# Where the row sums of a softmax get their small constant: GpSimd or ScalarE

## The chip, the cores and the metric
The kernel runs on one core of a Trainium2 chip. The core has a matrix engine (TensorE, PE in the profile, with PEld for the loading of its weights), VectorE (DVE), ScalarE (ACT), GpSimd (POOL) and SyncE (SP), which here issues most of the transfers between HBM and the core's memory SBUF. Each engine works through its own list of instructions in order, and waits on semaphores for the others. The metric is the device time of one execution, in microseconds; the median of several executions is what counts.

## The reference
An attention with a learned position bias is followed by a gated feed-forward layer. With 4 batches, 8 heads, S = 576 positions, heads of 64, and then 2304 tokens of width 512 with an inner width of 1536:
```python
scores = scale * np.matmul(q, k.transpose(0, 1, 3, 2))
...
scores = scores + bias.transpose(2, 0, 1)[None, :, :, :]
scores = scores - np.max(scores, axis=-1, keepdims=True)
attn = np.exp(scores)
attn = attn / (np.sum(attn, axis=-1, keepdims=True) + 1e-09)
return np.matmul(attn, v).astype(np.float32)
...
a = x @ w_a
b = x @ w_b
return (a * b @ w_out).astype(np.float32)
```
`x` is the attention's output, its heads side by side. The constant of the title is the 1e-9 that is added to each row's sum before the division.

## The kernel before
The attention is cut into 32 units (two chunks of positions, 4 batches, 4 pairs of heads) and these into 144 tiles, numbered n, of 128 rows by 576 columns of scores. One tile goes through these steps:

- TensorE multiplies q and k into a score buffer `qk` (L504 and L481 for the first 32 tiles, L490 after, L471 for the tail tile of a unit). One score buffer is used up to tile 50; after that two alternate.
- `soft1(n)`: VectorE's L518 adds the bias, scales, writes `p` to SBUF and keeps each row's minimum `mn`. With its read the score buffer is free for the next tile. Then ScalarE's L523 takes the exponential of `p` in place and leaves the row sums in `sm`; in the profile this is an ACTIVATE and an ACTIVATION_READ_ACCUMULATOR.
- `soft2(n)`, called one tile later in the program: GpSimd's L567 adds 1e-9 to `sm` and, from unit 12 (tile 48) on, divides by PS = 2^14; VectorE's L568 takes the reciprocal.
- Tiles 0 to 47: GpSimd's L573 multiplies `p` by the reciprocal, TensorE transposes it (L585, `tp`), ScalarE copies the result out (L590, L595).
- Tiles 48 to 143 (`split_turn`): GpSimd's L553 writes the normalised tile as 16-bit numbers `ph`, VectorE's two L555 write the remainder beside it, and SyncE issues a transposing transfer L561 of `ph` into `pt`.
- `pv` (L613) multiplies v and the transposed tiles of a unit; ScalarE's L626 and VectorE's L628 write the result into `x`.

The buffers `p` (three) and `sm`, `mn` (four each) rotate. Beside the attention TensorE does the feed-forward layer of the batch that is ready: the products `ab` (L715), which ScalarE scales (L723, `asb`), VectorE multiplies (L725, `g`), ScalarE and GpSimd split in two parts (L739 `gh`, L740 `gl`), and the output products (L764). Until some 37 us the position bias is built (`psta`), until some 165 us the weights are converted, by ScalarE (L264, L307), VectorE (L266, L267, L270) and GpSimd (L304, L308); the other half of the bias follows from 240 to 320 us. The attention ends at some 640 us, and the rest is feed-forward.

The order of TensorE's instructions is written by hand, by generators that are merged step by step (`tc.manual_schedule` for PE alone). The order of all other engines is set by the scheduler, which plays the program through with its own idea of each instruction's length and places each instruction when it takes its inputs to be ready. So a row added to one engine can change the order on the others.

Of the kernel before, what the change touches and what calls it, by code (L numbers as in the profile page):

```python
# [13 lines left out]
AF = mybir.ActivationFunctionType  # L14
ALU = mybir.AluOpType
# [15 lines left out]
PS = float(2 ** 14)  # L31
# [3 lines left out]
TILES = []  # L35
# [12 lines left out]
NF = 3 * NP  # L48
# [4 lines left out]
def attention_moe(ctx, tc, q0d, q1d, kd, vd, idn, wp, wa, wb, wo, lsw, lg, rl, out):  # L53
    nc = tc.nc
# [456 lines left out]
    def soft1(n):  # L511
        ps = st.pop(("qk", n))
        bt = st.pop(("bias", n))
        pool, bufs = att, 3
        p = pool.tile([128, S], F32, tag="p", name="p", bufs=bufs)
        mn = att.tile([128, 1], F32, tag="mn", name="mn", bufs=4)
        sm = att.tile([128, 1], F32, tag="sm", name="sm", bufs=4)
        ttr = nc.vector.tensor_tensor_reduce(  # L518
            out=p.rearrange("p (a n) -> p a n", a=2), in0=ps[:, :, :HB], in1=bt.rearrange("p (a n) -> p a n", a=2),
            op0=ALU.add, op1=ALU.min, scale=-0.125, scalar=3.0e38, accum_out=mn,  # L520
        )
        ttrs.append(ttr)
        exps.append(nc.scalar.activation(p, p, AF.Exp, bias=mn, scale=-1.0, accum_out=sm))  # L523
        st["p", n] = (p, sm)

    def pv_first(n, pool):
# [36 lines left out]
    def soft2(n):  # L563
        u, t = TILES[n]
        p, sm = st.pop(("p", n))
        rc = sm
        nc.gpsimd.tensor_scalar(out=sm, in0=sm, scalar1=1e-9, scalar2=1.0 / (PS if u >= NF else 1.0), op0=ALU.add, op1=ALU.mult)  # L567
        nc.vector.reciprocal(out=rc, in_=sm)  # L568
        if u >= NF:
            split_turn(n, p, rc)  # L570
            return
        pns.append(
            nc.gpsimd.tensor_scalar(out=p, in0=p, scalar1=rc, scalar2=1.0, op0=ALU.mult, op1=ALU.mult)  # L573
        )
        st["pn", n] = p
# [59 lines left out]
    def attn_steps():  # L635
        vgen = [None]
        for n in range(NT + 4):
# [7 lines left out]
            if n < NT:  # L645
                soft1(n)
# [47 lines left out]
            if 1 <= n <= NT:  # L694
                soft2(n - 1)
# [297 lines left out]
```

## Time and profile before

| | us |
|---|---|
| median of the runs (757.84 to 761.88) | 759.58 |
| the profiled execution, its span | 760.0 |
| TensorE busy | 704.6 |
| VectorE busy | 498.8 |
| ScalarE busy | 446.3 |
| GpSimd busy | 329.1 |

The span is that of one profiled execution, from its first instruction to its last. Read first the busy times, which tell which engine has little room; then the waits of that engine by what they waited for; then the timeline at the longest of them, from the waiting instruction backwards: the last thing in brackets is the idle time before an instruction and what ended it. An engine that is idle and not waited for costs nothing. The granted clock (PEclk) is TensorE's clock as a share of 2.4 GHz; its lower level is 1.2 GHz, half of that.

### The profile page before, as it was taken

How to read it: one execution, taken by the hardware profiler on the slowest of the kernel's cores; microseconds unless marked ns; L12 is line 12 of the kernel's file. 1: busy time of each engine (PE TensorE's matmuls, PEld its weight loads, DVE VectorE, ACT ScalarE, POOL GpSimd, SP SyncE). 2: the span in 40 equal slices, each digit the busy share in tenths (PEclk: the TensorE clock that was granted, in tenths of full speed). 3: DMA queues.
4: the chain of work that ended last, by engine and by line, in shares of the span. 5: the costliest groups of instructions: out<-in, count | busy, mean ns of one | idle time of the engine just before them, and what ended most of it. 6: DMA issues, size and time to landing. Idle time of an engine off the chain costs nothing.

```text
span 760.0 us, 15571 instructions
## 1 busy us (share of the span) xinstructions
PE 704.6 (93%) x5451; PEld 531.9 (70%) x5451; DVE 498.8 (66%) x1204; ACT 446.3 (59%) x1005; POOL 329.1 (43%) x477
## 2 busy tenths in 40 slices
PE   7778898899899999999889989999999999999997
PEld 2245465578787556687677768878778887888886
DVE  6767688849986578675788778878887772110200
ACT  6878887867875687754456456545655553422310
POOL 3437668855873133232545445524553452411200
PEclk9989999989999999999999999999999999999999
DMA  8898767477744888789999999999999974000001
GB/s 260 299 371 272 242 218 214 148 235 252 252 154 127 209 183 218 193 212 180 225 245 248 274 255 229 243 240 245 238 254 248 213 158 112 17 1 28 3 14 42
DMA packets 178163, 147.69 MB, mean 194 GB/s; under 512 B 125092, under 2 KB 138148, under 8 KB 178084
## 3 DMA queue, kind: packets, MB, share of 16 engines
q1 hardware_dynamic: 170928, 130.92, 68.2%
q10 hardware_dynamic: 5876, 10.93, 5.2%
q0 software_dynamic: 1280, 4.84, 1.8%
q8 instruction: 43, 0.70, 0.4%
q14 instruction: 36, 0.29, 0.1%
HBM read 101.15 MB, written 17.18 MB: 156 GB/s over the span
## 4 chain that ended last, share of the span: by engine, by line
PE 36%; issue 17%; DVE 15%; POOL 12%; ACT 10%; DMA 9%; SPq 1%; POOLq 0%; DVEq 0%; ACTq 0%
PE ab L715 15%; PE o L764 10%; POOL ph L553 5%; DMA bias<-bias_d 3%; POOL gl L740 3%; DMA pt<-ph 3%; DVE p L518 3%; PE pv L613 3%; PE psta L153 3%; DVE ph L555 2%; ACT p L523 2%; PE qk L490 2%; DVE w16t L267 2%; DVE wt L270 2%; POOL sm L567 2%
## 5 line engine op out<-in xcount | busy, mean ns | idle before, releaser
L715 PEld LDWEIGHTS <-w16t 128*128 128x128 f16 x2592 | 248.3, 98 | 47.2 <-issue 14.3
L715 PE MATMUL ab<-x,w16t 128*128 128x256 f16 x2304 | 273.2, 275 | 2.6 <-DVE g L725 1.0
L523 ACT ACTIVATE p<-p,mn 128x576 f32<-128x576 f32 x144 | 111.7, 776 | 138.7 <-DVE mn L518 117.4
L555 DVE SCALAR_TENSOR_TENSOR ph<-p,sm,ph 128x64 f16<-128x64 f32 x192 | 98.7, 554 | 34.1 <-POOL ph L553 32.0
L764 PE MATMUL o<-wos,gh 128*128 128x512 f32 x384 | 120.7, 395 | 0.0
L518 DVE CUSTOM_DVE_ANT_0 p<-qk,bias 128x576 f32<-128x576 f32 x144 | 107.7, 751 | 17.0 <-PE tp L585 5.6
L567 POOL TENSOR_SCALAR sm<-sm 128x1 f32<-128x1 f32 x144 | 42.1, 292 | 173.6 <-ACT p L523 169.3
L740 POOL TENSOR_TENSOR gl<-g,gh 128x256 fp32r<-128x256 f32 x96 | 75.1, 783 | 93.3 <-ACT gh L739 90.4
L553 POOL TENSOR_SCALAR ph<-p,sm 128x576 f16<-128x576 f32 x96 | 82.0, 854 | 52.5 <-DVE sm L568 39.7
L725 DVE SCALAR_TENSOR_TENSOR g<-ab,wv,asb 128x256 f32<-128x256 f32 x84 | 40.2, 479 | 73.0 <-ACT asb L723 73.0
L490 PE MATMUL qk<-ks,qs 128*128 128x288 f32 x384 | 72.9, 312 | 11.9 <-DVE mn L518 11.7
L764 PEld LDWEIGHTS o<-wos,gh 128*128 128x128 f32 x384 | 69.4, 188 | 16.0 <-issue 2.8
L764 PE MATMUL o<-wos,gl 128*128 128x512 f32 x192 | 75.0, 391 | 0.0
L490 PEld LDWEIGHTS qk<-ks,qs 128*128 128x128 f32 x384 | 55.8, 188 | 25.1 <-DVE mn L518 16.7
L739 ACT CAST gh<-g 128x256 fp32r<-128x256 f32 x96 | 38.3, 399 | 33.2 <-DVE g L725 32.8
L573 POOL TENSOR_SCALAR p<-p,sm 128x576 f32<-128x576 f32 x48 | 44.1, 920 | 28.5 <-DVE sm L568 23.9
L723 ACT ACTIVATE asb<-ab,wv 128x256 f32<-128x256 f32 x84 | 39.4, 469 | 27.6 <-PE ab L715 27.3
L568 DVE RECIPROCAL sm<-sm 128x1 f32<-128x1 f32 x144 | 23.1, 160 | 44.5 <-POOL sm L567 42.5
L407 DVE TENSOR_TENSOR ks<-rk,ks 64x576 fp32r<-64x576 f32 x48 | 44.9, 934 | 3.7 <-ACT ks L406 1.7
L613 PE MATMUL pv<-pt,vs 128*64 128x320 f16 (+1 forms) x560 | 41.8, 302 | 0.0
L585 PE MATMUL tp<-idn,p 128*128 128x128 f32 x240 | 37.1, 287 | 4.8 <-ACT ptf L590 4.0
L764 PEld LDWEIGHTS o<-wos,gl 128*128 128x128 f32 x192 | 36.0, 188 | 7.8
(102 smaller groups left out, 956.0 us busy)
## 6 DMA issues: line engine op xcount, KB each, us to landing
bias<-bias_d SPq DMA_DIRECT2D x128, 288.0 KB, 3.6
rv<-vd SPq DMA_DIRECT2D x32, 320.0 KB, 4.2
rk<-kd SPq DMA_DIRECT2D x24, 288.0 KB, 3.5
wraw<-wa SPq DMA_DIRECT2D x12, 512.0 KB, 7.0
wraw<-wb SPq DMA_DIRECT2D x12, 512.0 KB, 5.3
wraw<-wo SPq DMA_DIRECT2D x12, 512.0 KB, 4.5
bias_d<-bo ACTq DMA_DIRECT2D x20, 295.5 KB, 3.9
bias_d<-bo POOLq DMA_DIRECT2D x16, 295.5 KB, 7.0
```

The costliest lines, as they stand in the source:

```text
L407: nc.vector.tensor_tensor(out=ks[ol, j], in0=rk[sl], in1=ks[sl, j].bitcast(F32), op=ALU.subtract)
L490: nc.tensor.matmul(ps[:, hf, :HB], a, b[:, hf * HB:hf * HB + HB], start=(x == 0), stop=(x == len(prods) - 1))
L518: ttr = nc.vector.tensor_tensor_reduce(out=p.rearrange("p (a n) -> p a n", a=2), in0=ps[:, :, :HB], in1=bt.rearrange("p (a n) -> p a n", a=2),
L523: exps.append(nc.scalar.activation(p, p, AF.Exp, bias=mn, scale=-1.0, accum_out=sm))
L553: nc.gpsimd.tensor_scalar(out=ph[:, :S], in0=p, scalar1=rc, scalar2=1.0, op0=ALU.mult, op1=ALU.mult)
L555: ins = nc.vector.scalar_tensor_tensor(out=ph[:, o:o + c1 - c0], in0=p[:, c0:c1], scalar=rc, in1=ph[:, c0:c1], op0=ALU.mult, op1=ALU.subtract,
L567: nc.gpsimd.tensor_scalar(out=sm, in0=sm, scalar1=1e-9, scalar2=1.0 / (PS if u >= NF else 1.0), op0=ALU.add, op1=ALU.mult)
L573: nc.gpsimd.tensor_scalar(out=p, in0=p, scalar1=rc, scalar2=1.0, op0=ALU.mult, op1=ALU.mult)
L613: nc.tensor.matmul(ps[64 * j:64 * j + 64, o:o + N], v[:, j, :], p[:, j * N:j * N + N], start=(x == 0), stop=(x == len(prods) - 1),)
L715: nc.tensor.matmul(ab[:, j], w16[nm, f][:, pw, kk, :], xs[px][:, kk, :], start=(x % (3 * KC) == 0), stop=(x % (3 * KC) == 3 * KC - 1),)
L740: nc.gpsimd.tensor_tensor(out=gl, in0=g, in1=gh.bitcast(F32), op=ALU.subtract)
L764: nc.tensor.matmul(o, g[:, sl], wos[f][:, p], start=(f == 0 and x == 0), stop=(f == FC - 1 and x == 2))
```

## The change
In `soft1`, right after the exponential, ScalarE takes a copy of `sm` with a scale and a bias, so that `sm` holds (sum + 1e-9), divided by PS from tile 48 on. GpSimd's L567 in `soft2` is gone. The values are the same but for rounding. The program gives the copy one call behind the exponential; where it stands on ScalarE is the scheduler's choice, as before. Lines behind the new ones carry numbers that are one or two higher: the copy is L525, the reciprocal L569, the remainders L557, asb L724, g L726, gh L740.

```diff
--- before.py
+++ after.py
@@ -521,6 +521,8 @@
         )
         ttrs.append(ttr)
         exps.append(nc.scalar.activation(p, p, AF.Exp, bias=mn, scale=-1.0, accum_out=sm))
+        unit = PS if TILES[n][0] >= NF else 1.0
+        nc.scalar.activation(sm, sm, AF.Copy, bias=1e-9 / unit, scale=1.0 / unit)
         st["p", n] = (p, sm)
 
     def pv_first(n, pool):
@@ -564,7 +566,6 @@
         u, t = TILES[n]
         p, sm = st.pop(("p", n))
         rc = sm
-        nc.gpsimd.tensor_scalar(out=sm, in0=sm, scalar1=1e-9, scalar2=1.0 / (PS if u >= NF else 1.0), op0=ALU.add, op1=ALU.mult)
         nc.vector.reciprocal(out=rc, in_=sm)
         if u >= NF:
             split_turn(n, p, rc)
```

TensorE's order is the same before and after. ScalarE has 144 rows more and GpSimd 144 fewer; on VectorE about half of the rows move, most by one or two.

First VectorE, where the reduces of tiles 69 and 70 stand (`L518 ISA p,mn` is the reduce, `ISA mn` its read of the minimum, the two SCALAR_TENSOR_TENSOR rows on `ph` the remainders of one tile, here tile 68 first). Before:
```order
L518 ISA p,mn<-qk,bias 128x576
L518 ISA mn 128x1
L555 SCALAR_TENSOR_TENSOR ph<-p,sm,ph 128x64
L555 SCALAR_TENSOR_TENSOR ph<-p,sm,ph 128x512
L518 ISA p,mn<-qk,bias 128x576
L518 ISA mn 128x1
L568 RECIPROCAL sm<-sm 128x1
L725 SCALAR_TENSOR_TENSOR g<-ab,wv,asb 128x256
```
The reduce of tile 70 is the second one here; the remainders of tile 68 stand ahead of it. In the changed program the same place on VectorE reads:
```order
L518 ISA p,mn<-qk,bias 128x576
L518 ISA mn 128x1
L442 SCALAR_TENSOR_TENSOR vs<-rv,vs_452,vs 128x640
L569 RECIPROCAL sm<-sm 128x1
L518 ISA p,mn<-qk,bias 128x576
L518 ISA mn 128x1
L569 RECIPROCAL sm<-sm 128x1
L557 SCALAR_TENSOR_TENSOR ph<-p,sm,ph 128x64
L557 SCALAR_TENSOR_TENSOR ph<-p,sm,ph 128x512
L726 SCALAR_TENSOR_TENSOR g<-ab,wv,asb 128x256
```
The reduce of tile 70 stood behind the remainders of tile 68, and now stands ahead of them, behind a row on `vs` and the reciprocal of tile 68.

VectorE again, around the reduce of tile 40, among the rows that convert weights (`wu`, `wt`). Before:
```order
L568 RECIPROCAL sm<-sm 128x1
L267 SCALAR_TENSOR_TENSOR wu<-wraw,wu 128x512
L270 SCALAR_TENSOR_TENSOR wt<-wt,wu 128x512
L628 SCALAR_TENSOR_TENSOR x_2506<-pv,vs_2249,x_2505 128x256
L266 TENSOR_SCALAR wu<-wt 128x512
L267 SCALAR_TENSOR_TENSOR wu<-wraw,wu 128x512
L518 ISA p,mn<-qk,bias 128x576
L518 ISA mn 128x1
L725 SCALAR_TENSOR_TENSOR g<-ab,wv,asb 128x256
```
The reduce stands behind two rows on `wu`. In the changed program the same place on VectorE reads:
```order
L267 SCALAR_TENSOR_TENSOR wu<-wraw,wu 128x512
L270 SCALAR_TENSOR_TENSOR wt<-wt,wu 128x512
L629 SCALAR_TENSOR_TENSOR x_2508<-pv,vs_2251,x_2507 128x256
L569 RECIPROCAL sm<-sm 128x1
L266 TENSOR_SCALAR wu<-wt 128x512
L726 SCALAR_TENSOR_TENSOR g<-ab,wv,asb 128x256
L518 ISA p,mn<-qk,bias 128x576
L518 ISA mn 128x1
L267 SCALAR_TENSOR_TENSOR wu<-wraw,wu 128x512
```
The long row on `wu` from `wraw` has moved from ahead of the reduce to behind it; the reciprocal of tile 39 and the row on `g` have moved ahead of it.

Last ScalarE, at the exponentials of tiles 71 to 73 (`p,sm<-p,mn`; `ks` and `qs` are parts of the next unit's k and q). Before:
```order
L523 ACTIVATE p,sm<-p,mn 128x576
L723 ACTIVATE asb<-ab,wv 128x256
L739 CAST gh<-g 128x256
L523 ACTIVATE p,sm<-p,mn 128x576
L723 ACTIVATE asb<-ab,wv 128x256
L406 CAST ks<-rk 64x576 x2
L418 CAST qs<-rq 128x512
L523 ACTIVATE p,sm<-p,mn 128x576
```
Nothing stands here on `sm`, which GpSimd changes. In the changed program the same place on ScalarE reads:
```order
L523 ACTIVATE p,sm<-p,mn 128x576
L525 ACTIVATE sm<-sm 128x1
L740 CAST gh<-g 128x256
L724 ACTIVATE asb<-ab,wv 128x256
L523 ACTIVATE p,sm<-p,mn 128x576
L406 CAST ks<-rk 64x576 x2
L418 CAST qs<-rq 128x512
L740 CAST gh<-g 128x256
L525 ACTIVATE sm<-sm 128x1
L523 ACTIVATE p,sm<-p,mn 128x576
L724 ACTIVATE asb<-ab,wv 128x256
L525 ACTIVATE sm<-sm 128x1
```
The three copies `sm<-sm` are new: the first stands directly behind its exponential, the second four rows behind (the row on `ks` holds two instructions), the third two rows, each behind rows that the scheduler placed ahead of it.

## Rows read from the trace of the kernel before
**Rows 1.** The page, part 1: busy us, share, instructions of each engine.
```profile
PE 704.6 (93%) x5451; PEld 531.9 (70%) x5451; DVE 498.8 (66%) x1204; ACT 446.3 (59%) x1005; POOL 329.1 (43%) x477
```

**Rows 2.** Busy time by stretch: us, PE, PEld, DVE, ACT, POOL, granted clock, DMA.
```profile
345.00:440.00 95.00, 83.50 (x659) 66.10 (x657) 74.29 (x182) 50.88 (x116) 41.03 (x67) 0.98 1.10 236
440.00:645.00 205.00, 201.22 (x1660) 164.76 (x1661) 155.69 (x373) 110.70 (x262) 93.84 (x148) 0.99 0.99 222
```

**Rows 3.** Waits of TensorE, whole run: us in total, times, longest.
```profile
PE qk L490 <- DVE mn L518: 11.7, 11, 3.0
...
PE qk L481 <- DVE mn L518: 5.3, 3, 2.5
...
PE qk L504 <- DVE mn L518: 3.2, 3, 1.9
```

**Rows 4.** Groups by line: count | busy us, mean ns | idle before, releaser.
```profile
L523 ACT ACTIVATE p<-p,mn 128x576 f32<-128x576 f32 x144 | 111.7, 776 | 138.7 <-DVE mn L518 117.4
...
L523 ACT ACTIVATION_READ_ACCUMULATOR p<-p,mn 128x1 f32 x144 | 27.1, 188 | 0.0
...
L567 POOL TENSOR_SCALAR sm<-sm 128x1 f32<-128x1 f32 x144 | 42.1, 292 | 173.6 <-ACT p L523 169.3
...
L568 DVE RECIPROCAL sm<-sm 128x1 f32<-128x1 f32 x144 | 23.1, 160 | 44.5 <-POOL sm L567 42.5
```

**Rows 5.** Timeline of an undisturbed tile: start us, us, engine, line, operation [idle before].
```profile
575.61 0.19 ACT L523 ACTIVATION_READ_ACCUMULATOR p<-p,mn 128x1 f32 x1
...
575.88 0.19 POOL L567 TENSOR_SCALAR sm<-sm 128x1 f32<-128x1 f32 x1 [4.57 <-ACT p L523]
...
576.11 0.17 DVE L568 RECIPROCAL sm<-sm 128x1 f32<-128x1 f32 x1 [1.27 <-POOL sm L567]
```

**Rows 6.** Timeline, the same columns, a tile of the early stretch.
```profile
110.96 0.19 ACT L523 ACTIVATION_READ_ACCUMULATOR p<-p,mn 128x1 f32 x1
...
112.82 1.33 POOL L308 TENSOR_TENSOR w16t<-wt,w16t 128x512 f16<-128x512 f32 x1
...
114.24 0.51 POOL L567 TENSOR_SCALAR sm<-sm 128x1 f32<-128x1 f32 x1
```

**Rows 7.** Waits of 37 to 165 us: us in total, times, longest.
```profile
POOL sm L567 <- ACT p L523: 11.7, 11, 2.9
```

**Rows 8.** Timeline around TensorE's longest wait for L518 between 345 and 440 us.
```profile
362.25 0.74 POOL L553 TENSOR_SCALAR ph<-p,sm 128x576 f16<-128x576 f32 x1 [5.75 <-DMA pt<-ph]
363.03 0.95 DVE L555 SCALAR_TENSOR_TENSOR ph<-p,sm,ph 128x64 f16<-128x64 f32 x2 [3.47 <-POOL ph L553]
...
364.71 0.78 PE L490 MATMUL qk<-ks,qs 128*128 128x288 f32 x4 [2.98 <-DVE mn L518]
```

**Rows 9.** Busy time and granted clock (PEclk) of two stretches of 5 us.
```profile
200.00:205.00 5.00, 4.91 (x28) 3.90 (x29) 3.95 (x11) 4.93 (x12) 3.83 (x5) 0.66 0.85 261
...
365.00:370.00 5.00, 5.00 (x32) 3.52 (x35) 3.21 (x10) 3.85 (x9) 3.80 (x6) 0.66 1.03 184
```

**Rows 10.** Timeline around the wait at 200 us.
```profile
197.73 1.63 DVE L267 SCALAR_TENSOR_TENSOR wu<-wraw,wu 128x512 int32<-128x512 int32 x1
...
200.09 0.80 PE L490 MATMUL qk<-ks,qs 128*128 128x288 f32 x4 [2.56 <-DVE mn L518]
```

**Rows 11.** Timeline, two shorter waits of TensorE for L518.
```profile
380.94 0.53 PE L490 MATMUL qk<-ks,qs 128*128 128x288 f32 x2 [0.73 <-DVE mn L518]
...
539.55 0.66 PE L490 MATMUL qk<-ks,qs 128*128 128x288 f32 x3 [0.94 <-DVE mn L518]
```

**Rows 12.** Waits of ScalarE, whole run: us in total, times, longest.
```profile
ACT asb L723 <- PE ab L715: 29.6, 28, 2.1
```

**Rows 13.** Timeline, a unit's last transposing transfer and the matmul that reads it.
```profile
557.43 1.43 SPq L561 DMA_TRANSPOSE pt<-ph  x1
...
565.10 1.14 PE L613 MATMUL pv<-pt,vs 128*64 128x320 f16 x14
```

**Rows 14.** Timeline, TensorE's longest wait for a transfer after 345 us.
```profile
440.11 0.90 PE L471 MATMUL qk<-kt,qt 64*64 64x288 f32 x6 [3.31 <-DMA kt<-kd]
```

## The prediction

> **What bounds the kernel now.** I read the busy times of the engines first: TensorE is busy 704.6 of 760.0 us, VectorE 498.8, ScalarE 446.3, GpSimd 329.1 [rows 1]. So the order of TensorE's matmuls is nearly the time, and an edit on the other three engines is worth what it takes from, or adds to, the 55 us in which TensorE stands idle. By stretch, TensorE lacks 11.5 of 95 us between 345 and 440 us, but only 3.8 of 205 us between 440 and 645 us [rows 2]: gains are to be had in the first, hardly any in the second. Third, what those idle times wait for: the waits that the change can reach are those of a score matmul (qk) for VectorE's reduce L518, which must have read the one score buffer before it is written again. They come to 11.7 + 5.3 + 3.2 = 20.2 us [rows 3]. That is the ceiling of any gain (760.0 - 20.2 = 739.8); the matmuls' own waits for the small tile `sm` don't exist, since `sm` reaches TensorE only through a reciprocal, a multiply and a transpose.
>
> **What is removed and added.** Removed: 144 GpSimd instructions L567, 42.1 us, mean 292 ns; added: 144 ScalarE copies of a 128x1 tile [rows 4]. The trace has no such copy. Its nearest row is ScalarE's own read of the accumulator, 188 ns, also 128x1, so I take 0.19 us, 27 us in all. From below, an overlapping neighbour could hide half of it (ScalarE's next instruction starts some 0.1 us before the end of the one ahead), 14 us; from above I take the 292 ns of L567, 42 us. ScalarE rises from 446 to some 473 of 760 us, still far behind TensorE; by itself this is off the path. The Trainium skill, "ScalarE: Activation LUTs", section "What ACT_TABLE_LOAD costs", gives 186 ns plus 0.833 ns per element for an activation with immediate scale and bias, of which some 93 ns overlap back to back: an estimate of 144 x 0.094 = 13.5 us by that page; no row here shows this copy, and the sum would be the same.
>
> **Latency of one tile.** In an undisturbed tile the accumulator is read from 575.61 for 0.19 us, GpSimd's L567 runs from 575.88 for 0.19 and the reciprocal starts at 576.11 [rows 5]. A copy on ScalarE would take the same place at the same length: about 0.1 us saved at best. Where GpSimd has other work, L567 comes late: read at 110.96, but L567 starts at 114.24, behind the subtraction L308 (1.33 us) [rows 6]. Such lags fill the stretch up to 165 us, where L567 found its GpSimd idle and waiting for the exponential in only 11 of 32 tiles [rows 7]; added up over the 32 tiles they are 36 us (3.1 us at this one, 0.1 us where GpSimd is free). But the copy is not directly behind the exponential: the order of ScalarE has it there in 33 of 144 tiles, with 1.8 instructions between on the mean. In those first 32 tiles 62 instructions stand between, of some 0.5 to 0.8 us each (the exponential's 776 ns is the longest kind [rows 4]), so about 32 us plus what these wait for. One queue is exchanged for another: I take 0, bounds plus and minus 4 us.
>
> **What moves on VectorE.** The copy changes more than its own length. The scheduler now takes `sm` to be ready later and moves VectorE's reciprocals back by 1.15 rows and the two operations L555 by 1.11 rows on the mean, and the reduce L518 forward by 0.40. Where a reduce no longer stands behind an L555, it no longer waits for GpSimd either. The places with a wait of TensorE behind them:
> - Tile 70. GpSimd's L553 waited 5.75 us for a transfer, VectorE's L555 of tile 68 waited 3.47 us for that, the reduce of tile 70 stood behind it, and TensorE waited 2.98 us [rows 8]. In the new order that reduce stands before the L555 of tile 68. Minus 2.98. Right behind it the granted clock is 0.66 from 365 to 370 us [rows 9], that is, the lower of its two levels (1.2 GHz) for two thirds of the stretch; TensorE is busy all of it, so 0.34 x 5 = 1.7 us more go if the fall came from the wait. Together -4.7 (bounds -4.7 and 0).
> - Tiles 74 and 119. The reduce moves ahead of L555 of the tile before: the waits of 0.73 and 0.94 us [rows 11] go. -1.7.
> - Tile 40. TensorE waits 2.56 us for a reduce that starts behind the 1.63 us L267 [rows 10]. L267 moves behind the reduce; a 0.48 us multiply and a reciprocal of 160 ns move in front. -1.0 (bounds -1.6 and 0). The rest of this wait stays, and so does the low clock of 0.66 behind it [rows 9].
> Sum of the gains: -7.4 us.
>
> **What it costs.** (a) In eight places a reciprocal now stands ahead of a reduce that it stood behind (tiles 3, 23, 25, 31, 63, 95, 100, 120). With the copy in time that is 160 ns each [rows 4], 8 x 0.16 = +1.3. Where the copy stands behind a ScalarE instruction that waits for TensorE it is more: that wait is 29.6 / 28 = 1.06 us on the mean [rows 12], so at most 8 x 1.22 = +9.8. I take +1.3, since most of these waits meet copies elsewhere. (b) The L555 are later by a reduce of some 0.75 us, so the transposing transfers L561 are too. One of 557.43 ends its issue at 558.86 and the matmul pv that reads it starts at 565.10: 6.2 us [rows 13] cover it, cost 0; without that cover it would be 0.75 us per unit, 20 units, 15 us. (c) A gain before 440 us need not last: at 440.11 TensorE waits 3.31 us for the transfer of kt [rows 14]. If the transfers keep their pace, what was gained from 345 us on (4.7 + 0.7 = 5.4) is waited for there. Between all and nothing I take half, +2.7 (bounds 0 and 5.4).
>
> **Sum.** 760.0 - 7.4 + 1.3 + 2.7 = 756.6 for the profiled execution. Its span is 760.0 against a median of 759.58 of the runs, so 0.4 less for the median: **756.2**. By the bounds alone: all gains and no costs 759.6 - 8.0 - 4 = 747.6; no gains, and costs (a), (c) and the early tiles at their worst, 759.6 + 9.8 + 4 = 773.4.
>
> **Rivals.**
> Faster, 751: the gain isn't returned at kt, and GpSimd's absence helps VectorE. For it: L567 takes 0.51 us beside VectorE's work and 0.19 without [rows 5, 6], so the two engines slow each other, and L267 ahead of tile 40 took 1.63 us. The gains of 7.4, less 1.3, and the low clock at 200 us (1.7) going with a shorter wait, come to -7.8; some 0.1 us in each of ten reduces behind shared work make it -8.8: 759.6 - 8.8 = 750.8. Against it: GpSimd's large operations L553 and L573, which meet VectorE far longer, all stay. The Trainium skill, "GPSIMD Engine Reference", section "1. Specifications", says that GpSimd shares its SBUF interfaces with VectorE and contends with VectorE instructions of two SBUF inputs; the two lengths of L567 agree with it, and by that page alone one would expect this rival.
>
> Slower, 768: the copy is queued on the in-order ScalarE behind a row that waits for TensorE (asb from the product ab, or x from pv), the reciprocal waits for the copy, and the reduce of a later tile stands behind that reciprocal on VectorE, so TensorE waits for itself. In 57 tiles the copy has such a row ahead, in 24 of these a reduce stands within two rows behind the reciprocal. 24 x 1.06 = 25 us at the worst, half of it 12.7; with the gains left at -3.4 that gives 759.6 + 9.3 = 769, and some 768 if a part is covered. It decides from the point where the copy comes later than the time that the next qk has left. Against it: between 440 and 645 us TensorE is dense, and the exponential already waits on the same queue.
>
> No change, 759.6: the sum isn't taken from a queue at all, since 111 of 144 copies stand behind other work, and what is won at tile 70 is waited for at 440 us. It is also what comes out if the wait at tile 70 only moves to the next L555.
>
> **Chances.** The forecast (752 to 759.5) 0.48, faster rival 0.20, slower rival 0.18, no change 0.14. What a measurement of this kernel can tell from no change is 0.5%, 3.8 us: below 755.8 is faster, above 763.4 slower. Half of the forecast's chance lies below 755.8: faster 0.24 + 0.20 = 0.44; slower 0.18; same 0.24 + 0.14 = 0.38. The range that leaves out 2 in 10 reaches from the far side of the faster rival to the middle of the slower one: 748 to 767.
>
> **What would show it.** Right: no wait of some 3 us of qk at 365 us, and a granted clock of 1.0 there; the copies at about 0.19 us; VectorE's waits for `sm` now from ScalarE, of about the same total; the wait for kt at 440 us grown by 2 to 3 us. Wrong towards faster: the kt wait as before and TensorE's qk waits under 12 us. Wrong towards slower: new qk waits behind reciprocals that wait for the copy, with asb or x ahead of it on ScalarE; or pv waiting for transposes. A new fall of the granted clock, of the 1.7 us seen in [rows 9], can shift the time either way.

## The result, and the profile after

The changed kernel takes 767.12 us in the median of four runs, against 760.56 of the kernel before: ratio 1.0107, 95% interval 1.0070 to 1.0144 (here and below the ratio is estimated from the single runs, so it need not be the quotient of the two medians). Taken again in twelve runs (after_again) it was 765.56 against 760.25, ratio 1.0069 (1.0041 to 1.0096). So the change makes the kernel slower, by some 0.7 to 1.1 percent; the forecast was 756.2, with 748 to 767 as its range.

The profiled execution after has a span of 764.0 us, 4.0 above that of before. The medians are further apart than the spans, because the profiled execution of before was a long one: with what lies around its span (1.9 us) it took 761.88 us, the longest of its first four runs, while that of after, 765.77 us, was shorter than its median.

The first two lines are the page of after, the line of the span and part 1 (as [rows 1]); then two stretches (as [rows 2]; the columns after the length are PE, PEld, DVE, ACT, POOL, granted clock, DMA share, GB/s); then TensorE's waits (as [rows 3]: total, times, longest), and the group of the copies (as [rows 4]).
```profile
span 764.0 us, 15532 instructions
...
PE 704.0 (92%) x5451; PEld 533.5 (70%) x5451; DVE 501.6 (66%) x1204; ACT 464.0 (61%) x1149; POOL 277.3 (36%) x333
```
```profile
345.00:440.00 95.00, 85.86 (x692) 68.58 (x692) 79.42 (x188) 56.40 (x148) 29.16 (x40) 0.98 1.08 239
440.00:645.00 205.00, 195.29 (x1595) 161.38 (x1590) 153.01 (x365) 115.42 (x307) 74.14 (x95) 0.99 1.01 218
```
```profile
PE qk L490 <- DVE mn L518: 8.8, 9, 2.7
...
PE qk L471 <- DMA kt<-kd: 4.8, 2, 2.7
PE qk L481 <- DVE mn L518: 4.6, 3, 2.5
PE ab L716 <- DVE g L726: 3.7, 3, 1.7
...
PE tp L586 <- POOL p L574: 2.6, 1, 2.6
```
```profile
L525 ACT ACTIVATE sm<-sm 128x1 f32<-128x1 f32 x144 | 28.3, 198 | 1.4 <-ACT p L523 0.2
```
GpSimd is busy 277.3 us (329.1 before: L567 took 42.1 of the difference), and ScalarE has 28.3 us of copies, 198 ns each, as the sum had it. TensorE is as busy as before. Its two large waits for the reduce L518 fell, 11.7 and 5.3 us before [rows 3], 8.8 and 4.6 now. Larger are a wait of 2.6 us for GpSimd's multiplication (before 0.9), 3.7 us (before 1.0) for VectorE's g, and what the dense stretch from 440 to 645 us lost: TensorE is busy 195.29 of 205 us there, against 201.22.

Where the time goes is best read along the run. TensorE's 5,451 matmuls stand in the same order in all these kernels, so the start of one matmul in a trace, less its start in the trace of before, tells how far TensorE is behind (worked out from the timelines; negative is ahead). Besides the trace of after there is a second one of the same kernel (after_again), and two of the experiments below in the same order, without any copy: pool_in_new_order, in which GpSimd adds, and noop_new_order, in which no engine does.

| start in before, us | 58.3 | 204.0 | 350.7 | 369.7 | 405.5 | 472.1 | 522.8 | 555.3 | 573.0 | 607.8 | 619.5 |
|---|---|---|---|---|---|---|---|---|---|---|---|
| after, us later | 0.4 | 0.8 | 0.6 | -4.6 | -3.2 | -4.0 | -0.3 | -0.9 | 2.2 | 0.9 | 4.0 |
| after_again | -0.2 | 0.2 | 1.1 | -4.2 | -1.9 | -1.4 | 1.7 | 1.1 | 4.2 | 2.8 | 3.8 |
| pool_in_new_order | 1.7 | 3.1 | 2.2 | -2.7 | -1.6 | -0.7 | 2.9 | 2.6 | 6.0 | 4.6 | 5.4 |
| noop_new_order | -1.2 | -1.2 | -2.2 | -6.8 | -4.6 | -3.2 | -1.3 | -1.5 | -0.3 | -0.6 | 0.8 |

The gain around tile 70 is there: 5.2 us between 350.7 and 369.7 us, where the sum had 4.7. Most of it lasts until 472 us in the trace of after; then it goes in three steps, between 472 and 523, 555 and 573, and 608 and 620 us, and behind that nothing moves any more. Five places tell more. The first rows are ScalarE, VectorE, GpSimd and TensorE at tile 0 (start, length, engine, line; in brackets the idle time and what ended it):
```profile
38.36 0.19 ACT L523 ACTIVATION_READ_ACCUMULATOR p<-p,mn 128x1 f32 x1
...
40.38 0.33 ACT L525 ACTIVATE sm<-sm 128x1 f32<-128x1 f32 x2
...
41.49 0.22 DVE L569 RECIPROCAL sm<-sm 128x1 f32<-128x1 f32 x2
...
41.76 1.88 POOL L574 TENSOR_SCALAR p<-p,sm 128x576 f32<-128x576 f32 x2 [6.05 <-DVE sm L569]
...
42.97 0.77 PE L586 MATMUL tp<-idn,p 128*128 128x128 f32 x5 [2.58 <-POOL p L574]
```
Before, the reciprocal of tile 0 ran at 38.77 us and the first transposition tp started at 40.13. Now the first two copies stand behind two weight rows and the exponential of tile 1, the reciprocal stands behind the reduce of tile 2, and TensorE waits 2.58 us for GpSimd's multiplication. The wait is 2.58 us in pool_in_new_order and noop_new_order too, which have no copy, so it comes from the order, the reciprocal behind the reduce of tile 2. It costs nearly nothing in the end: before, TensorE waited for reduces a little later, and these waits are gone, so that at 58.3 us it is 0.4 us behind. Two of them, in the trace of before:
```profile
41.59 0.75 PE L504 MATMUL qk<-rkf,rqf 64*128 64x288 f32 x2 [0.74 <-DVE mn L518]
...
50.44 1.39 PE L504 MATMUL qk<-rkf,rqf 64*128 64x288 f32 x6 [1.90 <-DVE mn L518]
```

The second place is the tail tile of a unit, whose k comes by a transfer of its own (kt). SyncE's and TensorE's rows of before, and then of after:
```profile
383.23 1.32 SPq L427 DMA_DIRECT2D kt<-kd  x2
...
387.41 1.06 PE L471 MATMUL qk<-kt,qt 64*64 64x288 f32 x8 [1.19 <-DMA kt<-kd]
```
```profile
379.64 1.31 SPq L427 DMA_DIRECT2D kt<-kd  x2
...
383.68 1.21 PE L471 MATMUL qk<-kt,qt 64*64 64x288 f32 x8 [2.11 <-DMA kt<-kd]
...
437.71 0.71 PE L471 MATMUL qk<-kt,qt 64*64 64x288 f32 x6 [2.69 <-DMA kt<-kd]
```
TensorE came 4.65 us earlier than before (383.68 less the wait of 2.11 is 381.57, against 387.41 less 1.19, 386.22). The load of kt was issued 3.59 us earlier (379.64 against 383.23), so it is waited for longer: the gain is cut to 3.73 us (387.41 less 383.68). The next such wait, 2.69 us at 437.71, is 0.6 shorter than the 3.31 of [rows 14]. In all, the waits for kt are 4.8 us against 4.5 before (6.3 in after_again), so only a small part of the gain is given back there. Behind the first of them the granted clock is low, where it was 1.00 before; the fall that stood behind tile 70's wait [rows 9] has gone from there (1.00 from 365 to 370 us) and come back here:
```profile
385.00:390.00 5.00, 5.00 (x42) 3.47 (x39) 4.33 (x12) 3.43 (x13) 2.95 (x4) 0.66 1.07 275
```

The third place is the 3.7 us between 472 and 523 us: several waits of which before had none or 0.04 us, the two longest for the reduces of tiles 104 and 111:
```profile
484.82 0.80 PE L490 MATMUL qk<-ks,qs 128*128 128x288 f32 x4 [0.98 <-DVE mn L518]
...
509.21 0.71 PE L471 MATMUL qk<-kt,qt 64*64 64x288 f32 x8 [1.11 <-DVE mn L518]
```
The fourth is like that of tile 104, but larger, at the reduce of tile 124. VectorE's and TensorE's rows of before, and then of after:
```profile
553.62 0.16 DVE L568 RECIPROCAL sm<-sm 128x1 f32<-128x1 f32 x1
...
556.93 0.76 DVE L518 CUSTOM_DVE_ANT_0 p<-qk,bias 128x576 f32<-128x576 f32 x1
...
557.75 0.80 PE L490 MATMUL qk<-ks,qs 128*128 128x288 f32 x4 [1.15 <-DVE mn L518]
```
```profile
554.95 0.16 DVE L569 RECIPROCAL sm<-sm 128x1 f32<-128x1 f32 x1
...
556.54 0.95 DVE L557 SCALAR_TENSOR_TENSOR ph<-p,sm,ph 128x64 f16<-128x64 f32 x2 [0.65 <-POOL ph L555]
557.52 0.76 DVE L518 CUSTOM_DVE_ANT_0 p<-qk,bias 128x576 f32<-128x576 f32 x1
...
558.34 0.79 PE L490 MATMUL qk<-ks,qs 128*128 128x288 f32 x4 [2.64 <-DVE mn L518]
```
Before, the reciprocal of tile 123 stood ahead of three rows on x and GpSimd's pass was done in time. Now it stands behind them, the remainders wait 0.65 us for GpSimd, the reduce of tile 124 stands behind the remainders, and TensorE waits for it. At tile 111 the reduce itself has moved behind the first of two remainder rows, which waits 0.87 us for GpSimd. The same three waits are in the traces without a copy: 1.03, 1.15 and 2.86 us in pool_in_new_order, 0.48, 0.87 and 2.36 in noop_new_order.

The fifth is late, at a fetched g (gx), which ScalarE converts when its transfer has landed:
```profile
606.67 0.19 ACT L523 ACTIVATION_READ_ACCUMULATOR p<-p,mn 128x1 f32 x1
...
609.33 0.40 ACT L755 CAST gx<-gx 128x256 fp32r<-128x256 f32 x1 [2.48 <-DMA gx<-g_d]
609.65 0.20 ACT L525 ACTIVATE sm<-sm 128x1 f32<-128x1 f32 x1
...
609.88 0.16 DVE L569 RECIPROCAL sm<-sm 128x1 f32<-128x1 f32 x1 [2.92 <-ACT sm L525]
...
611.74 0.47 DVE L726 SCALAR_TENSOR_TENSOR g<-ab,wv,asb 128x256 f32<-128x256 f32 x1
...
612.26 2.78 PE L716 MATMUL ab<-x,w16t 128*128 128x256 f16 x24 [1.72 <-DVE g L726]
```
The copy of tile 137 stands behind the gx row, which waits for a transfer until 609.33. VectorE's reciprocal waits 2.92 us for the copy, the multiply g stands behind it on VectorE, and TensorE's products of the next block wait 1.72 us for g. This is the rival "slower" of the prediction with a transfer in the place of asb. But it comes and goes: in the second trace of the same kernel (after_again) this wait is not there. The next wait for g, 1.56 us here, is there too, with 1.38 us (before 0.34).

### The profile page after: what moved, and what is told of

It is laid out like the page before. It is cut to its first block, busy times and chain, and to the rows that moved or that the text cites. A ratio compares the mean times of both kernels' runs of the same rounds, so it can differ in the third digit from the quotient of the medians.

```text
span 764.0 us, 15532 instructions
## 1 busy us (share of the span) xinstructions
PE 704.0 (92%) x5451; PEld 533.5 (70%) x5451; DVE 501.6 (66%) x1204; ACT 464.0 (61%) x1149; POOL 277.3 (36%) x333
## 4 chain that ended last, share of the span: by engine, by line
PE 32%; issue 15%; DVE 11%; DMA 7%; ACT 6%; POOL 5%; SPq 1%; ACTq 0%; POOLq 0%; DVEq 0%
PE o L765 13%; PE ab L716 13%; POOL ph L555 4%; PE pv L614 3%; DVE p L518 3%; DVE ph L557 2%; DMA pt<-ph 2%; DMA bias<-bias_d 2%; ACT p L523 2%; PE qk L490 2%; PE psta L153 2%; POOL gl L741 1%; DVE ks L407 1%; DVE wu L267 1%; ACT ks L406 1%
## 5 line engine op out<-in xcount | busy, mean ns | idle before, releaser
L555 POOL TENSOR_SCALAR ph<-p,sm 128x576 f16<-128x576 f32 x96 | 74.5, 779 | 196.2 <-DVE sm L569 162.0
L557 DVE SCALAR_TENSOR_TENSOR ph<-p,sm,ph 128x64 f16<-128x64 f32 x192 | 108.8, 607 | 29.3 <-POOL ph L555 28.6
L518 DVE CUSTOM_DVE_ANT_0 p<-qk,bias 128x576 f32<-128x576 f32 x144 | 107.7, 750 | 29.1 <-PE tp L586 5.6
L726 DVE SCALAR_TENSOR_TENSOR g<-ab,wv,asb 128x256 f32<-128x256 f32 x84 | 40.2, 478 | 74.9 <-ACT asb L724 71.3
L740 ACT CAST gh<-g 128x256 fp32r<-128x256 f32 x96 | 38.3, 399 | 40.1 <-DVE g L726 39.6
L724 ACT ACTIVATE asb<-ab,wv 128x256 f32<-128x256 f32 x84 | 39.3, 467 | 28.1 <-PE ab L716 27.8
L407 DVE TENSOR_TENSOR ks<-rk,ks 64x576 fp32r<-64x576 f32 x48 | 37.5, 782 | 12.1 <-ACT ks L406 10.9
L586 PEld LDWEIGHTS tp<-idn,p 128*128 128x128 f32 x240 | 28.3, 147 | 20.9 <-issue 11.5
L614 PEld LDWEIGHTS <-vs 128*64 128x64 f16 x560 | 31.2, 112 | 13.2 <-issue 7.5
```

The lines of the kernel that those rows point to most:

```text
L407: nc.vector.tensor_tensor(out=ks[ol, j], in0=rk[sl], in1=ks[sl, j].bitcast(F32), op=ALU.subtract)
L518: ttr = nc.vector.tensor_tensor_reduce(out=p.rearrange("p (a n) -> p a n", a=2), in0=ps[:, :, :HB], in1=bt.rearrange("p (a n) -> p a n", a=2),
L555: nc.gpsimd.tensor_scalar(out=ph[:, :S], in0=p, scalar1=rc, scalar2=1.0, op0=ALU.mult, op1=ALU.mult)
L557: ins = nc.vector.scalar_tensor_tensor(out=ph[:, o:o + c1 - c0], in0=p[:, c0:c1], scalar=rc, in1=ph[:, c0:c1], op0=ALU.mult, op1=ALU.subtract,
L586: nc.tensor.transpose(tp[:, x, :], p[:, c0:c0 + 128], tab["idn"])
L614: nc.tensor.matmul(ps[64 * j:64 * j + 64, o:o + N], v[:, j, :], p[:, j * N:j * N + N], start=(x == 0), stop=(x == len(prods) - 1),)
```

## The experiments

The scheduler changes the order of four engines when one instruction changes, so an edit of the kernel tests two things at once. To part them, most kernels below have their order on ScalarE, VectorE, GpSimd and SyncE written down as lists ("old": that of the kernel before; "new": that of the changed kernel), TensorE's being fixed anyway:
```python
...
for e, perm in ORDERS.items():
    free = [i for i in traced if i.engine == e and id(i) not in mine]
    seq = [free[k] if k >= 0 else extras[-1 - k] for k in perm]
    for a, b in zip(seq, seq[1:]):
        tc.add_manual_dep(b, a.name, nosync, reason="order")
```
`extras` are the copies, or L567, and `mine` is the set of them; an edge orders two rows of one engine and adds no wait. Where only an order differs, the diff tells the move in words. The kernel before with its own order as lists wasn't run; copy_first_48 and idle_copy_late below, which have these lists, are at 1.0007 and 1.0010, so the lists by themselves cost nothing that shows.

### The order, and the engine that adds

**sub_in_old_order.** The change in the old order, each copy directly behind its exponential.
```diff
-Activation: order as scheduled with the copies
+Activation: old order, copy k behind exponential k
+DVE, Pool, SP: old order
```


> The changed kernel's instructions, but in the order of the kernel before on ScalarE, VectorE, GpSimd and SyncE; each copy directly behind its exponential. Theory O (the scheduler's new order costs the time, not the engine that does the addition): no cost left, 757 to 761 us, ratio 0.996 to 1.002. Theory Q (the copy stands late in ScalarE's queue): the same or better, 756 to 760, since no copy is late here. Theory E (27 us more of ScalarE's time are the cost): the loss stays, 765 to 768, ratio about 1.01.


766.46 us, ratio 1.0097 (1.0081 to 1.0114). The loss stays, so the new order is not the only thing that can cost; theory E was the one that had this.

**pool_in_new_order.** The kernel before in the changed kernel's order (GpSimd's left to the scheduler).
```diff
+Activation, DVE, SP: new order, without copies
```


> The kernel before (GpSimd adds the constant), but ScalarE, VectorE and SyncE in the order of the changed kernel. Theory O: the loss is there without the copy, 764 to 768 us, with the wait of some 2.6 us at 558 us and of 2.6 us at 43 us. Theory Q: no late copy, so 755 to 759 (the gain of 3 us at 365 us stays, the losses go). Theory E: 758 to 761.


767.39 us, ratio 1.0113 (1.0094 to 1.0132). So the loss is there without a copy as well: theory O. The waits that this theory expected are there, 2.58 us at tile 0 and 2.86 at tile 124.

**direct_copy.** The change in the new order, with all copies directly behind their exponentials.
```diff
 DVE, Pool, SP: new order
-Activation: copy k where the scheduler has it
+Activation: copy k behind exponential k
```


> The changed kernel in its own order on all engines, but each of the 144 copies moved directly behind its exponential on ScalarE; VectorE, GpSimd and SyncE as in the changed kernel. Theory Q: most of the loss goes, 759 to 762 us, and the two waits of TensorE for g at 612 and 617 us (3.3 us together in the changed kernel) with it. Theory O: what VectorE's order costs stays, 764 to 768. Theory E: 766 to 768.


772.64 us, ratio 1.0173 (1.0154 to 1.0192): slower than the changed kernel, outside every expectation. A late copy is not the general cause (theory Q fell), and an early one costs something of its own.

**noop_old_order** and **noop_new_order.** No engine adds anything; the two orders.
```diff
-        nc.gpsimd.tensor_scalar(out=sm, in0=sm, scalar1=1e-9, ...)
         nc.vector.reciprocal(out=rc, in_=sm)
...
-scalar2=1.0 / PS, op0=ALU.mult, op1=ALU.mult
+scalar2=1.0, op0=ALU.mult, op1=ALU.mult
...
-vsc[b][0] if u < NF else 1.0 / PS
+vsc[b][0] if u < NF else 1.0
```


> The order before on all engines, with the addition left out on every engine: 1e-9 isn't added, and the factor 2^14 of tiles 48 to 143 is left out, with the two later scalings by 2^-14 that undo it; the reciprocal takes the row sums as they are. Theory E: no copy, so no loss: 756 to 760 us. Theory A: the sums arrive earlier than the order was made for, as with the copy, and GpSimd's multiplications meet other work: 763 to 767. A third outcome, 750 to 755, would mean that the small instruction itself was on the path.


754.15 us, ratio 0.9941 (0.9914 to 0.9968). The fastest of all, and the third outcome: in the old order GpSimd's small instruction was itself on the path, with some 5 us.


> The changed kernel's order on all engines, with the addition left out on every engine (1e-9 and the factor 2^14 with the scalings that undo it are left out). Theory N (the new order costs by itself, whatever is done with the sums): 764 to 769 us, some 10 to 15 above the same instructions in the old order (754.2). Theory M (the new order is as good as the old one, and the copies in it cost what they cost in the old order): 752 to 757.


763.26 us, ratio 1.0049 (1.0023 to 1.0075): theory N in sign and, at 9 us above the old order, nearly in size.

**noop_own_order.** The same without lists.


> The addition left out on every engine as in the run with the old order (1e-9 and the factor 2^14 with its undoing are left out), and the order left to the scheduler. If a new order by itself costs some 1 percent, whatever is done with the sums (theory O): 764 to 769 us. If the order only fails where it was made for other instructions (theories E and A): 754 to 759, since one step of 0.3 us or more goes from each tile's chain.


759.35 us, ratio 1.0009 (0.9990 to 1.0028), a hair above the second range: against the kernel before nothing is lost, but the order that the scheduler makes for this program, a third one, gives back the 5 us that the missing instruction gained in the old order.

Put together, as ratios to the kernel before:

| order | no addition | GpSimd adds | ScalarE adds, copy directly behind | ScalarE adds, as scheduled |
|---|---|---|---|---|
| old | 0.9941 | 1 | 1.0097 | |
| new | 1.0049 | 1.0113 | 1.0173 | 1.0069 and 1.0107 |

Down a column the new order costs 1.1 points without any addition, 1.1 with GpSimd, 0.8 with direct copies. Along the new row ScalarE's copy, where the scheduler has put it, is no dearer than GpSimd's instruction (their intervals overlap). Added up, GpSimd's instruction is worth 0.6 points in either order, ScalarE's copy as scheduled 0.2 to 0.6, and the new order 1.1. So the loss of the change is that of its order. Which engine's part of the order costs it was not tested: the lists of ScalarE, VectorE and SyncE were always changed together. How the order loses shows along the run in the table above, whose steps are there without a copy, and in the waits of TensorE with no addition in the new order:
```profile
PE qk L490 <- DVE mn L518: 7.9, 8, 2.8
...
PE qk L471 <- DMA kt<-kd: 5.4, 2, 2.7
...
PE qk L471 <- issue: 2.1, 1, 2.1
```
The gain at tile 70 is there as in the changed kernel, and goes as there: a part at kt, 5.4 us in two waits (4.5 before), and in a wait on TensorE's own side ("issue", nothing that the profile shows; none before), and a part behind 472 us, where the waits for the reduces of tiles 104, 111 and 124 are (0.48, 0.87 and 2.36 us; 0, 0.04 and 1.15 before). It belongs to the order, and its return too.

### What a copy costs on ScalarE

**idle_copy_old_order** and **idle_copy_late.** GpSimd adds as before, in the old order; ScalarE also copies each `sm` into a tile that nobody reads: directly behind the exponential, or directly ahead of the next one.
```diff
         exps.append(nc.scalar.activation(p, p, AF.Exp, ..., accum_out=sm))
+        jk = att.tile([128, 1], F32, tag="jk", name="jk", bufs=4)
+        nc.scalar.activation(jk, sm, AF.Copy, bias=1e-9, scale=1.0)
...
-        rc = sm
-        nc.gpsimd.tensor_scalar(out=sm, in0=sm, scalar1=1e-9, ...)
-        nc.vector.reciprocal(out=rc, in_=sm)
+        rc = att.tile([128, 1], F32, tag="rc", name="rc", bufs=4)
+        nc.gpsimd.tensor_scalar(out=rc, in0=sm, scalar1=1e-9, ...)
+        nc.vector.reciprocal(out=rc, in_=rc)
```


> The kernel before in its own order, GpSimd still adding the constant (into a tile of its own, rc), plus 144 copies of sm on ScalarE directly behind the exponentials into a tile that nobody reads. Theory E (the copies' 27 us on ScalarE delay what stands behind them): the loss of 7 us of the old-order substitution is there, 764 to 768 us. Theory A (the loss comes from when the sums arrive at VectorE and GpSimd, not from ScalarE's load): 758 to 761.


770.73 us, ratio 1.0138 (1.0106 to 1.0170): theory E, and dearer than it expected.


> As the run with the idle copies in the old order (GpSimd adds the constant; 144 copies on ScalarE that nobody reads), but each copy directly ahead of the next tile's exponential instead of directly behind its own. Theory E1 (any 0.2 us of ScalarE costs, by its sum): 768 to 772 us again. Theory E2 (what costs is the 0.23 us by which the copy holds up the rows right behind the exponential, asb, gh and the parts of x, ks and vs, on which VectorE waits; ahead of an exponential ScalarE mostly waits for VectorE's reduce anyhow): 758 to 763.


760.84 us, ratio 1.0010 (0.9983 to 1.0037). The same 144 copies cost 10 us or nothing, by their place: theory E2. Its mechanism is in ScalarE's rows, at tile 72, of the kernel before, of sub_in_old_order and of idle_copy_late in turn:
```profile
371.73 0.19 ACT L523 ACTIVATION_READ_ACCUMULATOR p<-p,mn 128x1 f32 x1
...
371.83 0.46 ACT L723 ACTIVATE asb<-ab,wv 128x256 f32<-128x256 f32 x1
```
```profile
371.05 0.18 ACT L523 ACTIVATION_READ_ACCUMULATOR p<-p,mn 128x1 f32 x1
371.27 0.20 ACT L525 ACTIVATE sm<-sm 128x1 f32<-128x1 f32 x1
371.38 0.46 ACT L724 ACTIVATE asb<-ab,wv 128x256 f32<-128x256 f32 x1
```
```profile
370.23 0.20 ACT L525 ACTIVATE jk<-sm 128x1 f32<-128x1 f32 x1
...
370.80 0.78 ACT L523 ACTIVATE p<-p,mn 128x576 f32<-128x576 f32 x1 [0.37 <-DVE mn L518]
...
371.48 0.19 ACT L523 ACTIVATION_READ_ACCUMULATOR p<-p,mn 128x1 f32 x1
371.57 0.46 ACT L725 ACTIVATE asb<-ab,wv 128x256 f32<-128x256 f32 x1
```
Without a copy the row asb starts 0.10 us after the read of the accumulator, whose end it overlaps (371.83 less 371.73); with the copy between them 0.33 us after (371.38 less 371.05), since the copy itself starts only 0.22 us after the read. Each direct copy holds up what stands behind it by 0.23 us. Ahead of the next exponential ScalarE has time: in the third fence asb follows the read by 0.09 us. The waits of TensorE for the reduce rise with the direct idle copies and not with the late ones; first direct, then late:
```profile
PE qk L490 <- DVE mn L518: 18.8, 16, 3.3
```
```profile
PE qk L490 <- DVE mn L518: 12.0, 12, 2.5
```
18.8 us against 12.0, and 11.7 before [rows 3]: in the substitution itself they are 15.0 us (sub_in_old_order) and 17.2 (copy_last_96). That each wait of a chain through ScalarE and VectorE's in-order queue gets a little longer is how I read it; the rows show it at tile 72 only. ScalarE has idle time enough by its share, 175.65 of 300 us busy from 345 to 645 us in the direct run; it isn't idle at that place.

**copy_first_48** and **copy_last_96.** The substitution in the old order for a part of the tiles only.
```diff
+        if u < NF:   # copy_first_48; u >= NF in copy_last_96
+            nc.scalar.activation(sm, sm, AF.Copy, ...)
```


> The old order on all engines, ScalarE's copy directly behind the exponential for tiles 0 to 47 only, GpSimd's instruction kept for tiles 48 to 143. Theory E: a loss where ScalarE is busiest, in the first 240 us, where it is busy 79 percent between 37 and 165 us: 763 to 766. Theory A: a third of the tiles, 760 to 763, and less if the loss belongs to the transposing transfers, which only tiles 48 to 143 have.


759.31 us, ratio 1.0007 (0.9985 to 1.0029): nothing, less than either theory had.


> The old order on all engines, ScalarE's copy directly behind the exponential for tiles 48 to 143 only, GpSimd's instruction kept for tiles 0 to 47: the complement of the run of the first 48, which was at 759.3. If the two parts add up: all of the loss, 765 to 768 us. If the loss needs both (an early delay that shifts the later stages against their transfers): 759 to 763.


769.02 us, ratio 1.0106 (1.0068 to 1.0144). All of the loss belongs to tiles 48 to 143, not to the early stretch in which ScalarE is busiest. In these tiles VectorE makes two more passes per tile and reduces stand behind them; that this is why is likely, but no run shows it.

**copy_one_row_later** and **idle_copy_one_row.** Old order, copies of tiles 48 to 143 one row later where that row is gh, ks, x, asb or vs.
```diff
-Activation: exp k, copy k, gh
+Activation: exp k, gh, copy k
```


> The changed kernel's instructions in the order of the kernel before; the copies of tiles 48 to 143 stand one row later on ScalarE than in the first such run (behind the gh, ks, x, asb or vs row that follows the exponential, 77 tiles; directly behind the exponential in the others). Theory E2 (the rows right behind the exponential must not be held up): a part of the 7 us comes back, 761 to 765 us. Theory A2 (the sum has to arrive early as well, so that a later copy costs on VectorE what it saves on ScalarE): 766 to 770.


765.98 us, ratio 1.0090 (1.0063 to 1.0118), not to be told from the 1.0097 of the direct place; theory A2 to within 0.02 us of its range.


> The run with the idle copies in the old order (GpSimd adds the constant; 144 copies on ScalarE that nobody reads), the copies of tiles 48 to 143 one row later (behind the gh, ks, x, asb or vs row that follows the exponential, 77 tiles). If only the row right behind the exponential must not be held up: 759 to 763 us. If any row before the next exponential's wait must not be: 766 to 771, as with the copies directly behind.


763.02 us, ratio 1.0051 (1.0023 to 1.0079). One row later frees more than half of the idle copies' cost (1.0138), and nothing of the real copies'. The two differ in that VectorE waits for the real ones: what ScalarE saves, the later sum takes. That is theory A2, by exclusion, and not shown in rows; a place that is late enough for ScalarE and early enough for VectorE wasn't found in the old order.

### Single places in the new order

**gx_two_copies, new_order_mended, new_order_mended_4.** The changed kernel in its order, with two, three and four copies moved, and one and two reciprocals.
```diff
 gx_two_copies
-Activation: exp 137, gx, copy 137 ... exp 142, asb, gx, copy 142
+Activation: exp 137, copy 137, gx ... exp 142, copy 142, asb, gx
 new_order_mended
+Activation: exp 0, copy 0      DVE: reduce 1, reciprocal 0
 new_order_mended_4
+Activation: exp 123, copy 123  DVE: reciprocal 123, x, xt, xt
```


> The changed kernel in its own order, with two of the 144 copies moved by one row each on ScalarE: those of tiles 137 and 142, from behind a gx instruction that waits for a transfer to directly behind their exponentials. Theory Q: the waits of TensorE for g at 612 and 617 us, 1.72 and 1.56 us, go: 763 to 765 us. Theory O: VectorE's and TensorE's orders put something else late there, 766 to 768.


765.01 us, ratio 1.0081 (1.0066 to 1.0097): the wait for g at gx is gone, the other (1.55 us) is still there, so that one does not come from gx. But the wait at gx is also gone in after_again, where no copy was moved, so its going can't be put down to the move. The interval doesn't part this run from the changed kernel.


> The changed kernel in its own order, with three copies (tiles 0, 137, 142) moved directly behind their exponentials on ScalarE and the reciprocal of tile 0 moved back ahead of the reduce of tile 2 on VectorE. If the losses that the trace shows at 43 us (2.6) and at 612 and 617 us (3.3) are single places in the new order: 761 to 764 us, and no wait of over 1.5 us at these places. If other work waits there in their place: 765 to 768.


763.72 us, ratio 1.0047 (1.0022 to 1.0072). The wait of 2.58 us at tile 0 is gone; in its place TensorE waits 0.95 and 1.33 us for reduces at 41.72 and 43.81 us (0.74 and 0.59 in before). A wait of 1.35 us for g stays.


> The mended new order with a fourth place: tile 123's copy directly behind its exponential and its reciprocal ahead of the three x rows on VectorE, as in the order before. If the wait of 2.64 us at 558 us is a single place too: 1 to 3 us less than with three places (763.7), 761 to 763. If the copy's hold-up of the x rows takes it back: 764 to 766.


762.50 us, ratio 1.0026 (1.0003 to 1.0048). The wait at tile 124 fell only from 2.6 to 2.09 us, but behind it the granted clock is 1.00 from 557.5 to 565 us, where the changed kernel has 0.77. The interval reaches those of the changed kernel by a hair (1.0048 against 1.0041) and of the kernel with three moves, so the single steps are not shown; that four moves among some 2,900 rows bring most of the loss back is likely, but not shown.

**after_again.** The changed kernel in more runs.


> The changed kernel once more, in more rounds, since the first comparison had four runs: ratio 1.007 to 1.014, 765 to 770 us.


765.56 us, ratio 1.0069 (1.0041 to 1.0096), as told above.

## Why the prediction was wrong

**The step that failed** is the price of the new order. The prediction had in its own words that reciprocals and remainders move back by more than a row on the mean, and put the cost of that to the reduces at eight reciprocals (1.3 us) and the rest at nothing; its terms for the order, -7.4 + 1.3 + 2.7, make -3.4 us. With GpSimd still adding, the order of the changed kernel measured +8 us (pool_in_new_order, 767.39 against 759.27), and with no addition +9 (763.26 against 754.15). The traces show it in places where TensorE hardly waited before, so that no row called attention to them: the reduces of tiles 64, 86, 103, 111, 123 and 131 stand behind more remainder rows than before (counted in the two timelines of VectorE), and the reciprocals of tiles 103 and 123 behind rows on x. TensorE's waits for the reduces of tiles 104, 111 and 124 went from 0, 0.04 and 1.15 us to 0.98, 1.11 and 2.64.

**The base of the sum** holds: the profiled span of 760.0 was 0.4 above the median of 759.58, and 759.58 less 3.4 is the 756.2 of the forecast.

**Removed and added** was right as a length, 0.198 us where 0.19 was taken, and wrong in what it does. "By itself this is off the path", argued from ScalarE's share of 59 percent, fails in the old order: a direct copy holds up the rows behind it by 0.23 us and costs 7 us in all (sub_in_old_order), 10 when GpSimd's instruction stays (idle_copy_old_order). The bound from above, 42 us of busy time, was never carried to the sum, since a share of busy time was taken as cover. In the changed kernel itself the exchange of the two instructions comes out about even, since the scheduler put most copies elsewhere.

**The latency of one tile** was taken as an exchange of two queues, 0 plus or minus 4. As an exchange that held: TensorE is 0.8 us behind at 204 us, and copy_first_48 is at 1.0007. What it missed is that the small instruction is on the path at all: left out in the old order, it gives 5 us back (noop_old_order).

**What moves on VectorE** was right in its mechanism and nearly in its size where it was read: the wait of 2.98 us at tile 70 went, and TensorE gained 5.2 us there. The fall of the granted clock went from there as well, but one of the same 0.66 stands 20 us later, behind kt. At tiles 74 and 119 waits of 0.26 and 0.29 us are left of 0.73 and 0.94. At tile 40 the gain of 1.0 did not come: TensorE waits 2.7 us there, 2.56 before.

**What it costs**: (a) counted reciprocals that move ahead of a reduce, and not remainders that do, nor reciprocals that move back. (b) held for the transposing transfers in the changed kernel, of which TensorE waits for none by more than 0.7 us. (c) took half of the gain to be waited for at kt by 440 us; the waits for kt grew by 0.3 us (1.8 in after_again). The gain was given back, but for the most part elsewhere and behind 472 us.

**The rivals.** "Slower" gave 768, near the 767.12 and 765.56 measured, but that is in the main luck: its mechanism, a copy queued behind a row that waits, shows at gx in one of two traces, while the same order without any copy loses as much. Direct copies are slower still (direct_copy). "No change" had the gain at tile 70 given back at 440 us, which is not where it goes. "Faster" is refuted: GpSimd's absence did not speed VectorE up. Its remainder passes take 607 ns on the mean, 554 before, in the group rows of before and then of after (count | busy us, mean ns | idle before):
```profile
L555 DVE SCALAR_TENSOR_TENSOR ph<-p,sm,ph 128x64 f16<-128x64 f32 x192 | 98.7, 554 | 34.1 <-POOL ph L553 32.0
```
```profile
L557 DVE SCALAR_TENSOR_TENSOR ph<-p,sm,ph 128x64 f16<-128x64 f32 x192 | 108.8, 607 | 29.3 <-POOL ph L555 28.6
```
The difference goes with the order and not with GpSimd's load: the same passes take 603 ns in the new order with L567 (pool_in_new_order) and 554 in the old order without it (sub_in_old_order). No rival said that the order as a whole is worse, which it is, by 1.1 points, with or without the addition.

**What stays open** is how much of the order's 8 us each of its moved rows costs, on which engine, and how much of it is a lower granted clock behind the new waits (last section); and which of the rows behind a copy must not be held up.

## What to carry to other kernels

In a program whose scheduler orders four engines by its own idea of lengths, the price of an edit can be the price of the order that comes with it, as here: hold the order and change the instruction, then hold the instruction and change the order, before either is called the cause. An engine that is idle 40 percent of the time is not idle at the place where the new instruction stands; ask which row is next on that engine, who waits for that row, and whether the engine itself waits anywhere later in the same tile, where the instruction would be free. The fastest version here adds nothing at all: in the old order the kernel without the addition is at 0.9941; each exponential's row has a largest element of 1, so in 32-bit arithmetic its sum doesn't change by 1e-9.

## What the runs showed of the hardware

A 128x1 activation of 198 ns directly behind the read of an accumulator holds up its successors by 0.23 us, more than its own length: it starts 0.04 us after the read's end, while a row that doesn't need the read starts 0.09 us before that end (rows at tile 72). The Trainium skill, "ScalarE: Activation LUTs", section "What ACT_TABLE_LOAD costs", has 186 ns plus 0.833 ns per element for an activation with immediate scale and bias, by estimate 187 ns for this copy, and an overlap of some 93 ns back to back. The 198 ns are 11 longer; the overlap shows in asb, which starts 0.09 us before the copy's end, and not in the copy behind the read that it needs.

The granted clock goes to the lower of its two levels for a while behind some of TensorE's short waits, as at 365 us in before [rows 9] and at 385 us in after. First the stretch behind tile 0's wait in the trace of after, then two stretches of before:
```profile
42.50:52.50 10.00, 8.66 (x41) 5.78 (x43) 5.39 (x14) 7.06 (x18) 2.60 (x4) 0.57 1.03 402
```
```profile
42.50:50.00 7.50, 4.74 (x38) 3.07 (x38) 3.82 (x10) 5.96 (x14) 2.37 (x6) 1.00 1.03 406
50.00:57.50 7.50, 6.71 (x38) 4.49 (x38) 6.46 (x20) 5.24 (x12) 2.33 (x5) 0.59 0.87 295
```
The clock is 0.57 over 10 us in after, in which TensorE is busy 8.66; in before it is 1.00 until 50 us and 0.59 in the next 7.5. The wait of 2.58 us isn't needed for it: new_order_mended_4, without that wait, has 0.57 from 42.5 to 52.5 us as well. In the twelve later runs of the changed kernel the granted clock is 0.980 in the mean, in the 23 runs of before beside them 0.987: 0.007 x 764 = 5 us, if TensorE were busy all the time. The loss there is 5.3 us, so up to nearly all of it can be waits that cost a second time, through the clock; the runs don't part the two. With four moves (new_order_mended_4) the mean is 0.985, as in before beside it. It is not the cause in general: the direct idle copies lost 10 us at a mean of 0.986.
